# Routing attention and MLP mixer: seven block products for the second token product of two batches, the rounding's integer addition on VectorE, and the sums of the channel weights in slices

## The chip, the cores and the metric

The kernel runs on one core of one Trainium2 chip. The metric is the device time of one launch in microseconds (us), as the median of several launches. A core has a matrix engine (TensorE, "PE" in the profile; its weight loads are listed as "PEld"), a vector engine (VectorE, "DVE"), a scalar engine (ScalarE, "ACT"), GpSimd ("POOL") and a queue that issues transfers (SyncE, "SP"). Each engine works through its own list of instructions in the order of the program; semaphores hold an instruction until what it needs is done.

## The reference

Two stages, 4 batches, all in float32:

```python
# attention: 8 heads, 768 tokens, 64 per head, 16 clusters
mask   = q_assign[:, :, :, None] == k_assign[:, :, None, :]     # same cluster?
scores = np.where(mask, 0.125 * q @ k^T, -1e9)
attn   = softmax(scores) @ v                                    # (4, 8, 768, 64)
x      = attn.transpose(0, 2, 1, 3).reshape(4, 768, 512)

# mixer: w_tok1 (768, 256), w_tok2 (256, 768), w_ch1 (512, 1536), w_ch2 (1536, 512)
h  = np.maximum(x.transpose(0, 2, 1) @ w_tok1, 0.0) @ w_tok2    # over the tokens
u  = x + h.transpose(0, 2, 1)
h2 = np.maximum(u @ w_ch1, 0.0) @ w_ch2                         # over the channels
return u + h2
```

The four weights arrive as 64-bit floats and are turned into 32-bit floats on the chip ("rounding" in the kernel).

## The kernel before

The program is written in the order in which each engine executes it. Its stages: attention of 16 pairs of heads (with the rounding of `w_tok1`, `w_tok2` and `w_ch1` spread over it), the token products (with the rounding of `w_ch2`), then the channel products of the four batches.

The channel products are already done with seven block products in place of eight: both factors are cut into 2 by 2 blocks, sums and differences of blocks (`S1` to `S4` on the left, `T1` to `T4` on the right) are formed on VectorE, and seven products give the four blocks of the result. The helper that orders one chunk of it:

```python
    def chunk(n, product, done, last=False):
        def ptile(tag):                    # ps_m has 2 buffers for each tag
            return pools["ps_m"].tile([P, n], F32, tag=tag, name="p" + tag)

        X = ptile("X")
        product(X, "A11", "B11", True)
        if late:
            late.pop()()                   # the last product of the chunk before
        done("p1", X)
        Z = ptile("Z")
        product(Z, "S1", "T1", True)
        done("p5", Z)
        Y = ptile("Y")

        def product_y():
            product(Y, "A12", "B21", True)
            done("c11", Y)

        def product_z():
            product(Z, "S4", "B22", False) # on top of what stands in Z
            done("c12", Z)

        between = [product_y, product_z]
        if not last:
            between.pop(0)()
        product(X, "S2", "T2", False)      # on top of p1, once that was read
        done("u2", X)
        between.pop(0)()
        product(X, "S3", "T3", False)
        done("c22", X)
        if last:
            between.pop(0)()

        def end():
            product(X, "A22", "T4", False)
            done("c21", X)

        late.append(end)
```

A `done` reads the matmul's result out of PSUM; the next product into the same tile waits for it. The rounding of a piece of 512 columns of a weight (`raw` has the low and the high words side by side):

```python
        def scalar_part(p):                                   # ScalarE
            p["h"] = tmp("wh", U32, p["n"])
            nc.scalar.activation(out=p["h"].bitcast(F32), in_=p["hi"].bitcast(F32), func=ACT.Abs)
            p["up"] = tmp("wup", I32, p["n"])
            nc.scalar.activation(out=p["up"], in_=p["lo"], func=ACT.Copy, scale=float(2.0**-29))

        def rest(dst, p):
            h = p["h"]
            nc.vector.tensor_scalar(...)                      # L210
            nc.vector.tensor_scalar(...)                      # L215
            T = tmp("wT", U32, p["n"])                        # one buffer
            nc.vector.scalar_tensor_tensor(out=T, in0=p["hi"], ...)   # L220
            T, up = T.bitcast(I32), p["up"]
            if len(dst.shape) == 3:                           # tok2 only
                T, up = (y.rearrange("t (p j) -> t p j", j=NJ) for y in (T, up))
            nc.gpsimd.tensor_tensor(out=dst.bitcast(I32), in0=T, in1=up, op=ALU.add)   # L227
```

The token products and the sums of the left channel weights:

```python
    def tok1(b, t):
        if t == 0:
            h1s[b] = tokpool.tile([P, NT, DM], F32, name="h1", bufs=2)
        pf = mtile([P, DM], "ph1")
        for j in range(NJ):                                   # 6 matmuls, 512 wide
            nc.tensor.matmul(pf, lhsT=W["tok1"][:, j, t * P : (t + 1) * P], rhs=xs[b][:, j], ...)
        relu(h1s[b][:, t], pf)                                # VectorE and ScalarE in turn

    def tok2(b, j):
        pu = mtile([P, DM], "pu")
        for t in range(NT):                                   # 2 matmuls, 512 wide
            nc.tensor.matmul(pu, lhsT=W["tok2"][:, t, j], rhs=h1s[b][:, t], ...)
        nc.vector.tensor_tensor(out=xs[b][:, j], in0=pu, in1=xs[b][:, j], op=ALU.add)  # L539

    def left_weights():
        # A11..A22: four blocks of w_ch1, each 2 x 768 columns per partition
        yield lambda: add(A["S1"], A["A21"], A["A22"])        # 1536 elements each
        yield lambda: sub(A["S2"], A["S1"], A["A11"])
        yield lambda: sub(A["A21"], A["A11"], A["A21"])
        yield lambda: sub(A["S4"], A["A12"], A["S2"])
```

The token stage, and the first channel products:

```python
    ends = [lambda t=t: tok1(0, t) for t in range(NT)]
    for b in range(B):
        if b + 1 < B:
            ends += [lambda b=b, t=t: tok1(b + 1, t) for t in range(NT)]
        ends += [lambda b=b, j=j: tok2(b, j) for j in range(NJ)]
    # ... attention ...
    for m in range(9):
        ends.pop(0)()
        if m == 1:
            pair_put(NPAIR - 1)       # last heads' result into x, on ScalarE
            pair_out(NPAIR - 1)       # divided by the softmax sums, on VectorE
        if m % 3 == 2:
            rounding(2)
    # ...
    beside = weights + list(left_weights())
    turning = list(u_steps(0))        # u of batch 0, turned, for the channel products
    while ends:
        for _ in range(-(-len(beside) // len(ends))):
            beside.pop(0)()
        ends.pop(0)()
        if len(ends) < 18 and turning:
            turning.pop(0)()
    u_sums()                          # T1..T4 of u, on VectorE
    # ...
    beside = list(right_weights())    # four sums of w_ch2, 1536 elements each
    for b in range(B):
        for part in range(2):
            for i in range(3):
                ch1_chunk(part, i)
                # ...
                for _ in range(2):
                    if beside:
                        beside.pop(0)()
            for i in range(3):
                # ...
                ch2_chunk(b, part, i)
```

Of the kernel before, what the change touches and what calls it, by code (L numbers as in the profile page):

```python
# [48 lines left out]
def kernel(  # L49
# [131 lines left out]
    def weight_steps(pool, W, names):  # L181

        def tmp(name, dt, n):  # L190
            bufs = 1 if name == "wT" else 2
            return pool.tile([P, WMAX], dt, tag=name, name=name, bufs=bufs)[:, 0:n]

        def load_bits(src, p):
            n = p["n"] = src.shape[1]
            raw = pool.tile([P, WMAX, 2], U32, tag="raw", name="raw", bufs=3)[:, 0:n]
            nc.sync.dma_start(raw.rearrange("p n two -> p (n two)"), src.bitcast(U32))
            p["lo"], p["hi"] = raw[:, :, 0], raw[:, :, 1]

        def scalar_part(p):  # L200
# [9 lines that stand above are left out]
            nc.vector.tensor_scalar(  # L210
                out=h.bitcast(F32), in0=h.bitcast(F32), scalar1=TINY, scalar2=HUGE,
                op0=ALU.max, op1=ALU.min,
            )

            nc.vector.tensor_scalar(  # L215
                out=h, in0=h, scalar1=0x07FFFFFF, scalar2=3,
                op0=ALU.bitwise_and, op1=ALU.logical_shift_left,
            )
            T = tmp("wT", U32, p["n"])
            nc.vector.scalar_tensor_tensor(  # L220
                out=T, in0=p["hi"], scalar=0xC0000000, in1=h,
                op0=ALU.bitwise_and, op1=ALU.bitwise_or,
            )
            T, up = T.bitcast(I32), p["up"]
            if len(dst.shape) == 3:
                T, up = (y.rearrange("t (p j) -> t p j", j=NJ) for y in (T, up))
            nc.gpsimd.tensor_tensor(out=dst.bitcast(I32), in0=T, in1=up, op=ALU.add)  # L227

        pieces = list(weight_pieces(W, names))
        parts = [{} for _ in pieces]  # L230
        for i in range(len(pieces) + 2):

            def step(i=i):
                if 2 <= i:
                    rest(pieces[i - 2][0], parts[i - 2])
                if 1 <= i <= len(pieces):
                    scalar_part(parts[i - 1])
                if i < len(pieces):
                    load_bits(pieces[i][1], parts[i])

            yield step
# [262 lines left out]
        state.pop(g)  # L504


    turns = [0, 0]

    def relu(dst, src):
        turns[0] += 1  # L510
        if turns[0] % 2:
            nc.vector.tensor_scalar_max(out=dst, in0=src, scalar1=0.0)
        else:
            nc.scalar.activation(out=dst, in_=src, func=ACT.Relu)

    def mtile(shape, name):
        turns[1] += 1
        return pools["ps_m"].tile(shape, F32, tag="XZ"[turns[1] % 2], name=name)

    h1s = {}  # L520

# [4 lines that stand above are left out]
        for j in range(NJ):  # L526
            nc.tensor.matmul(  # L527
                pf, lhsT=W["tok1"][:, j, t * P : (t + 1) * P], rhs=xs[b][:, j],
                start=(j == 0), stop=(j == NJ - 1),
            )  # L530
        relu(h1s[b][:, t], pf)

    def tok2(b, j):
        pu = mtile([P, DM], "pu")
        for t in range(NT):
            nc.tensor.matmul(  # L536
                pu, lhsT=W["tok2"][:, t, j], rhs=h1s[b][:, t], start=(t == 0), stop=(t == NT - 1)
            )
        nc.vector.tensor_tensor(out=xs[b][:, j], in0=pu, in1=xs[b][:, j], op=ALU.add)  # L539

# [12 lines left out]
    def left_weights():  # L555

        w = W["ch1"]
        half = DCH // 2
        A = {
            f"A{i + 1}{j + 1}": w[:, 2 * j : 2 * j + 2, half * i : half * i + half]  # L560
            for i in range(2)
            for j in range(2)
        }
        extra = pools["wsums"].tile([P, 3, 2, half], F32, name="w1s")
        A["S1"], A["S2"], A["S4"] = (extra[:, i] for i in range(3))
        yield lambda: add(A["S1"], A["A21"], A["A22"])
        yield lambda: sub(A["S2"], A["S1"], A["A11"])
        yield lambda: sub(A["A21"], A["A11"], A["A21"])
        yield lambda: sub(A["S4"], A["A12"], A["S2"])
        A["S3"] = A["A21"]  # L570
        pools["A"] = A

    def right_weights():

        w = W["ch2"]
        B_ = {
            f"B{i + 1}{j + 1}": w[:, 6 * i : 6 * i + 6, 256 * j : 256 * j + 256]
            for i in range(2)
            for j in range(2)
        }  # L580
        extra = pools["wsums"].tile([P, 3, NCT // 2, DM // 2], F32, name="w2s")
        B_["T1"], B_["T2"], B_["T4"] = (extra[:, i] for i in range(3))
        yield lambda: sub(B_["T1"], B_["B12"], B_["B11"])
        yield lambda: sub(B_["T2"], B_["B22"], B_["T1"])
        yield lambda: sub(B_["B12"], B_["B12"], B_["B22"])
        yield lambda: sub(B_["T4"], B_["B21"], B_["T2"])
        B_["T3"] = B_["B12"]
        pools["B"] = B_
# [45 lines left out]
    def chunk(n, product, done, last=False):  # L634


        def ptile(tag):
# [5 lines that stand above are left out]
            late.pop()()  # L643
# [11 lines that stand above are left out]
            product(Z, "S4", "B22", False)  # L655
# [6 lines that stand above are left out]
        product(X, "S2", "T2", False)  # L662
# [9 lines that stand above are left out]
            done("c21", X)  # L672

        late.append(end)

    def ch1_chunk(part, i):

# [160 lines left out]

    begin()
    weights = list(weight_steps(stage, W, ("tok1", "tok2", "ch1")))  # L840
    ends = [lambda t=t: tok1(0, t) for t in range(NT)]
    for b in range(B):
        if b + 1 < B:
            ends += [lambda b=b, t=t: tok1(b + 1, t) for t in range(NT)]
        ends += [lambda b=b, j=j: tok2(b, j) for j in range(NJ)]

    def route_on(g):
        route(g)
        route_big(g)
# [46 lines left out]

    ps_sc_stack.close()
    pools["ps_m"] = pool("ps_m", 2, space=PSUM)
    for m in range(9):
        ends.pop(0)()  # L900
        if m == 1:
            pair_put(NPAIR - 1)
            pair_out(NPAIR - 1)
        if m % 3 == 2:
            rounding(2)
    assert not state
    attention.close()
    pools["wsums"] = pool("wsums", 1, side="right")
    pools["u"] = pool("upool", 1, side="right")
    beside = weights + list(left_weights())  # L910
    turning = list(u_steps(0))
    while ends:
        for _ in range(-(-len(beside) // len(ends))):
            beside.pop(0)()
        ends.pop(0)()
        if len(ends) < 18 and turning:
            turning.pop(0)()
    u_sums()
    staging.close()
    tokens.close()  # L920
    pools["mlp"] = pool("mlp", 1)
    beside = list(right_weights())
    for b in range(B):
        for part in range(2):
            for i in range(3):
                ch1_chunk(part, i)
                if part == 1 and b + 1 < B:
                    if i == 0:
                        turning = list(u_steps(b + 1))
                    if i < 2:  # L930
                        turning.pop(0)()
                for _ in range(2):
                    if beside:
                        beside.pop(0)()
            for i in range(3):
                if b == B - 1 and part == 1 and i == 2:
                    both = fits_load()
# [226 lines left out]
```

## Time and profile before

| | |
|---|---|
| time, median of 3 | 845.06 us (844.65 to 845.54) |
| profiled execution | 843.0 us |
| attention, 0 to 318 us | TensorE busy 314.87 us of it |
| token products, 318 to 401.5 us | TensorE busy 82.75 us of 83.5 |
| channel products of batch 0, 401.5 to 456 us | TensorE busy 54.14 us of 54.5, VectorE 30.10 us |
| the rest, 456 to 843 us | TensorE busy 381.25 us of 387 |
| VectorE over the whole span | busy 501.5 us (59%) |

A line of the groups reads: line of the program, engine, operation, what it writes and reads with shapes, the count; then total busy time and mean duration of one in ns; then the idle time of the engine before them, and what ended it. One float32 matmul is two records of TensorE, which overlap. A line of the timeline reads: start in us, length in us, engine, line, operation, operands, count, and in brackets how long the engine had been idle and what released it.

### The profile page before, as it was taken

The numbers are of one execution on the slowest core, as the hardware profiler recorded it, in microseconds if no ns is written. First come the engines' busy times: TensorE is split into PE (matmuls) and PEld (weight loads), VectorE is DVE, ScalarE is ACT, GpSimd is POOL, SyncE is SP. The second block draws the span as 40 slices with busy tenths as digits, with TensorE's granted clock in tenths as the row PEclk, the third lists the DMA queues.
The fourth block names the chain that finished last, engine by engine and source line by source line (L and its number), as shares of the span: only waits on it lengthen the run. The fifth ranks groups of instructions, "written<-read, shape, count | busy, mean of one in ns | idle before, by whom it ended". The sixth has DMA issues, their size and how long they took to land.

```text
span 843.0 us, 10784 instructions
## 1 busy us (share of the span) xinstructions
PE 833.0 (99%) x4102; PEld 506.3 (60%) x4102; DVE 501.5 (59%) x848; ACT 375.0 (44%) x570; POOL 45.7 (5%) x40
## 2 busy tenths in 40 slices
PE   8999999999999999999999999999999999999997
PEld 4444444444444444444577686785876867768676
DVE  6879898989898862893653434423454333443342
ACT  5678677777777762453210352103612035220210
POOL 1001010101101000330000000000000000000000
PEclk9999999999999999999999999999999999999999
DMA  9887566867775312541000050000310012200001
GB/s 152 152 149 150 114 138 136 164 129 156 149 134 122 57 44 71 170 101 28 0 1 1 19 107 26 0 1 19 87 46 0 1 19 47 85 1 0 1 17 63
DMA packets 183963, 60.19 MB, mean 71 GB/s; under 512 B 172768, under 2 KB 176864, under 8 KB 183904
## 3 DMA queue, kind: packets, MB, share of 16 engines
q1 hardware_dynamic: 182304, 59.04, 33.2%
q8 instruction: 34, 0.56, 0.3%
q10 hardware_dynamic: 1600, 0.39, 0.2%
q14 instruction: 25, 0.20, 0.1%
HBM read 34.64 MB, written 6.29 MB: 49 GB/s over the span
## 4 chain that ended last, share of the span: by engine, by line
PE 92%; DVE 6%; issue 0%; ACT 0%; DMA 0%; DVEq 0%
PE sc L422 18%; PE pX L740 15%; PE pX L689 15%; PE av L447 13%; PE pZ L689 7%; PE pZ L740 7%; PE ph L527 4%; PE pY L740 4%; PE pY L689 4%; PE pu L536 3%; PE small L483 1%; DVE wh L215 1%; PE small L302 1%; DVE wT L220 1%; DVE wh L210 1%; DVE sum L437 1%
## 5 line engine op out<-in xcount | busy, mean ns | idle before, releaser
L429 ACT ACTIVATE ex<-sc 128x768 f32<-128x768 f32 x192 | 149.2, 812 | 27.6 <-PE sc L422 16.1
L422 PE MATMUL sc<-qkT 64*128 64x384 f32 x768 | 155.1, 482 | 0.0
L437 DVE TENSOR_TENSOR sum<-sum,ex 128x768 f32<-128x768 f32 x128 | 127.7, 997 | 27.4 <-ACT ex L429 15.2
L447 PE MATMUL av<-ex,va 128*64 128x384 f32 x768 | 127.4, 488 | 0.0
L447 PEld LDWEIGHTS av<-ex,va 128*64 128x64 f32 x768 | 53.7, 137 | 71.7 <-issue 67.9
L422 PEld LDWEIGHTS sc<-qkT 64*128 64x128 f32 x768 | 68.4, 187 | 36.3 <-issue 35.5
L697 ACT COPY p<-pX 128x384 f32<-128x384 f32 x24 | 11.4, 475 | 139.5 <-PE pX L689 121.2
L689 PE MATMUL pX<-uT,wc 128*128 128x384 f32 x192 | 67.4, 487 | 0.0
L422 PE MATMUL sc<-ohT 64*128 64x384 bf16 x384 | 63.3, 324 | 0.5 <-DVE ohT L394 0.2
L689 PEld LDWEIGHTS pX<-uT,wc 128*128 128x128 f32 x192 | 36.2, 190 | 24.7 <-issue 1.0
L454 ACT COPY avrows<-av 128x768 uint16<-128x768 uint16 x32 | 25.5, 798 | 47.1 <-PE av L447 47.1
L227 POOL TENSOR_TENSOR wc<-wT,wup 128x512 int32<-128x512 int32 x24 | 33.0, 1376 | 191.3 <-DVE wT L220 191.3
L527 PE MATMUL ph<-x,wt 128*128 128x512 f32 x96 | 41.9, 594 | 0.8 <-DVE x L539 0.8
L610 ACT COPY uT<-ucols 128x768 uint16<-128x768 uint16 x32 | 33.7, 1052 | 19.7 <-DMA ucols<-urows 19.7
L536 PE MATMUL pu<-h,wt 128*128 128x512 f32 x96 | 41.7, 592 | 0.0
L422 PEld LDWEIGHTS <-ohT 64*128 64x128 bf16 x384 | 20.1, 94 | 35.9 <-issue 11.1
L553 DVE TENSOR_TENSOR c<-pZ,u 128x384 f32<-128x384 f32 x24 | 13.4, 557 | 46.9 <-PE pZ L689 46.9
L708 ACT ACTIVATE hA<-hA 128x384 f32<-128x384 f32 x24 | 12.6, 523 | 63.4 <-DVE hA L553 63.4
L553 DVE TENSOR_TENSOR x<-pX,x 128x256 f32<-128x256 f32 x24 | 10.2, 423 | 42.8 <-PE pX L740 42.8
L689 PE MATMUL pZ<-uTs,w1s 128*128 128x384 f32 x96 | 35.0, 487 | 0.4 <-DVE uTs L550 0.4
L740 PE MATMUL pX<-wc,hA 128*128 128x256 f32 x144 | 35.0, 379 | 0.0
L740 PE MATMUL pZ<-w2s,hS 128*128 128x256 f32 x144 | 35.0, 379 | 0.0
(121 smaller groups left out, 1222.3 us busy)
## 6 DMA issues: line engine op xcount, KB each, us to landing
raw<-in_moe_w_ch_dram SPq DMA_DIRECT2D x24, 512.0 KB, 4.2
va<-in_v_dram SPq DMA_DIRECT2D x16, 384.0 KB, 3.6
out_dram<-x SPq DMA_DIRECT2D x24, 256.0 KB, 2.2
qk<-in_k_dram SPq DMA_DIRECT2D x60, 96.0 KB, 3.9
qk<-in_q_dram SPq DMA_DIRECT2D x60, 96.0 KB, 3.5
raw<-in_moe_w_tok_dram SPq DMA_DIRECT2D x3, 512.0 KB, 4.3
raw<-in_moe_w_tok_dram SPq DMA_DIRECT2D x4, 384.0 KB, 3.8
ucols<-urows SPq DMA_TRANSPOSE x32, 2.8
```

Source lines behind the costliest of these rows:

```text
L227: nc.gpsimd.tensor_tensor(out=dst.bitcast(I32), in0=T, in1=up, op=ALU.add)
L422: nc.tensor.matmul(sc[:, h, 0:HS], lhsT=src[rows, 1, j], rhs=src[rows, 0, js], start=start, stop=not start,)
L429: nc.scalar.activation(out=ex, in_=sc[:, :, 0:HS], func=ACT.Exp, scale=SM_SCALE)
L437: nc.vector.tensor_tensor(out=acc, in0=acc if j > 1 else st["ex", qh, 0], in1=st["ex", qh, j], op=ALU.add)
L447: nc.tensor.matmul(av[h * D : (h + 1) * D], lhsT=st["va"][:, h, j], rhs=ex[:, h], start=(j == 0), stop=(j == NJ - 1),)
L454: nc.scalar.copy(out=st["rows"][:, qh], in_=av.bitcast(U16).rearrange("p (t w) -> p w t", w=2))
L527: nc.tensor.matmul(pf, lhsT=W["tok1"][:, j, t * P : (t + 1) * P], rhs=xs[b][:, j], start=(j == 0), stop=(j == NJ - 1),)
L536: nc.tensor.matmul(pu, lhsT=W["tok2"][:, t, j], rhs=h1s[b][:, t], start=(t == 0), stop=(t == NT - 1))
L553: nc.vector.tensor_tensor(out=dst, in0=a, in1=b, op=ALU.add)
L610: nc.scalar.copy(out=out, in_=pools.pop(("ucols", i)).rearrange("p w j t -> p w (j t)"))
L689: nc.tensor.matmul(psum, lhsT=A[a][:, k, c * P : (c + 1) * P], rhs=R[r][:, k], start=start and k == 0, stop=k == 1, skip_group_check=not s ...
L740: nc.tensor.matmul(psum, lhsT=h2[a][:, k, i * P : (i + 1) * P], rhs=Bw[w][:, 3 * part + k], start=start and k == 0, stop=k == 2, skip_grou ...
```

## The change

It does three things.

- **The second token product.** The output of two batches is cut into 2 by 2 blocks (halves of the tokens by the two batches), the inner dimension of 256 into two, and the product is done with seven block products in place of eight, through the `chunk` helper. It is meant to save matmuls. For it, sums of the blocks of `w_tok2` are formed once (`token_weights`) and sums of the two batches' hidden layers for each pair of batches (`token_sums`). Both batches' first products now stand ahead of the second, and the relu is on ScalarE alone.
- **The rounding's integer addition** is on VectorE in place of GpSimd, except for `w_tok2`. It is meant to keep the two engines out of each other's way.
- **The sums of `w_ch1`** are formed in slices of 128 columns: the first during the second token product, the other five between the chunks of batch 0's channel products. They are meant to leave VectorE free in the token stage.

```diff
             T, up = T.bitcast(I32), p["up"]
+            engine = nc.vector
             if len(dst.shape) == 3:
+                engine = nc.gpsimd
                 T, up = (y.rearrange("t (p j) -> t p j", j=NJ) for y in (T, up))
-            nc.gpsimd.tensor_tensor(out=dst.bitcast(I32), in0=T, in1=up, op=ALU.add)
+            engine.tensor_tensor(out=dst.bitcast(I32), in0=T, in1=up, op=ALU.add)
...
-        relu(h1s[b][:, t], pf)
-
-    def tok2(b, j):
-        pu = mtile([P, DM], "pu")
-        for t in range(NT):
-            nc.tensor.matmul(
-                pu, lhsT=W["tok2"][:, t, j], rhs=h1s[b][:, t], start=(t == 0), stop=(t == NT - 1)
-            )
-        nc.vector.tensor_tensor(out=xs[b][:, j], in0=pu, in1=xs[b][:, j], op=ALU.add)
+        nc.scalar.activation(out=h1s[b][:, t], in_=pf, func=ACT.Relu)
...
+    def left_sums(A, part):
+        a = {name: part(x) for name, x in A.items()}
+        yield lambda: add(a["S1"], a["A21"], a["A22"])
+        yield lambda: sub(a["S2"], a["S1"], a["A11"])
+        yield lambda: sub(a["S3"], a["A11"], a["A21"])
+        yield lambda: sub(a["S4"], a["A12"], a["S2"])
+
+    def left_chunk(c):
+        return left_sums(pools["A"], lambda x: x[:, :, c * P : (c + 1) * P])
+
+    def token_weights():
+        w = W["tok2"]
+        A = pools["AT"] = {
+            f"A{i + 1}{j + 1}": w[:, j, HJ * i : HJ * i + HJ] for i in range(2) for j in range(2)
+        }
...
+        return left_sums(A, lambda x: x)
+
+    def token_sums(b, t):
+        R = pools["RT"] = {f"B{j + 1}{k + 1}": h1s[b + k][:, j] for j in range(2) for k in range(2)}
...
+        if t == 0:
+            sub(R["T1"], R["B12"], R["B11"])
+        else:
+            sub(R["T2"], R["B22"], R["T1"])
+            sub(R["T3"], R["B22"], R["B12"])
+            sub(R["T4"], R["B21"], R["T2"])
...
+    def tok2_chunk(b, i):
+        A, R = pools["AT"], pools["RT"]
...
+        to = {"p1": "c11", "p5": "c22", "u2": "c12"}
+
+        def product(psum, a, r, start):
+            nc.tensor.matmul(psum, lhsT=A[a][:, i], rhs=R[r], start=start, stop=True, ...)
+
+        def done(name, psum):
+            x = u[to.get(name, name)]
+            add(x, psum, x)
+
+        chunk(DM, product, done, i == HJ - 1)
+        if i == HJ - 1:
+            late.pop()()
...
+    others = weights
+    for b in (0, 2):
+        for i in range(2):
+            for t in range(NT):
+                tok1(b + i, t)
+                if (b, i) == (2, 0):
+                    turning.pop(0)()
+                if (b, i, t) == (0, 0, 1):
+                    pair_put(NPAIR - 1)
+                    pair_out(NPAIR - 1)
...
+                    for sums_of in token_weights():
+                        sums_of()
+                if i == 1:
+                    if t == 0:
+                        token_sums(b, 0)
+                    beside((2, 1)[t])             # steps of the rounding
+                    if t == 1:
+                        token_sums(b, 1)
+                else:
+                    beside(1 if b == 0 else (2, 2)[t])
+                if (b, i) == (2, 1):
+                    turning.pop(0)()
+        for i in range(HJ):
+            tok2_chunk(b, i)
+            if b == 0 and i == HJ - 1:
+                turning = list(u_steps(0))
+            if b == 2:
+                for _ in range(2):
+                    turning.pop(0)()
+                if i == 1:
+                    left_weights()
+                    others = list(left_chunk(0))
+                if i >= 1:
+                    beside(2)
     u_sums()
...
+    others = list(right_weights())
...
                 ch1_chunk(part, i)
...
-                for _ in range(2):
-                    if beside:
-                        beside.pop(0)()
+                if b == 0:
+                    c = 3 * part + i + 1
+                    for sums_of in left_chunk(c) if c < NCT // 2 else ():
+                        sums_of()
+                    beside(min(len(others), 1 + (i == 1)))
```

## The prediction

> **What bounds the kernel now.** I read the page's busy times first, then the stages by windows, then the groups of the token products, and last the timeline around the hand-overs that the change touches.
>
> ```profile
> PE 833.0 (99%) x4102; PEld 506.3 (60%) x4102; DVE 501.5 (59%) x848; ACT 375.0 (44%) x570; POOL 45.7 (5%) x40
> ```
>
> The windows, with the busy time of TensorE, its weight loads, VectorE, ScalarE and GpSimd in each, then the granted clock:
>
> ```profile
> 318.00:401.50 83.50, 82.75 (x194) 36.48 (x194) 52.19 (x71) 33.02 (x47) 15.44 (x12) 1.00 0.36 93
> 401.50:456.00 54.50, 54.14 (x207) 38.85 (x206) 30.10 (x50) 8.48 (x18) 0.00 (x0) 1.00 0.00 0
> ```
>
> TensorE is busy 99% of the span, also within the token stage and batch 0's channel products, at the full granted clock (1.00). So time goes only if TensorE gets fewer matmuls, and every new wait of TensorE is paid in full.
>
> ```profile
> L527 PE MATMUL ph<-x,wt 128*128 128x512 f32 x96 | 41.9, 594 | 0.8 <-DVE x L539 0.8
> L536 PE MATMUL pu<-h,wt 128*128 128x512 f32 x96 | 41.7, 592 | 0.0
> ```
>
> 96 records of the second product are 48 matmuls. The timeline steps 1.715 us from one eviction to the next, for two matmuls: 0.858 us each. The stage needs 96 x 0.858 = 82.3 us and runs from 317.93 to 401.46: only 1.2 us of it is lost.
>
> ```profile
> 329.03 1.95 ACT L472 COPY x<-avcols 128x768 uint16<-128x768 uint16 x2
> ...
> 330.10 0.56 DVE L498 TENSOR_TENSOR x<-x,rcps 128x384 f32<-128x384 f32 x1 [6.02 <-ACT x L472]
> ...
> 361.31 0.42 DVE L210 TENSOR_SCALAR wh<-wh 128x512 f32<-128x512 f32 x1
> 361.53 1.32 POOL L227 TENSOR_TENSOR wc<-wT,wup 128x512 int32<-128x512 int32 x1 [1.67 <-DVE wT L220]
> 361.76 1.37 DVE L215 TENSOR_SCALAR wh<-wh 128x512 uint32<-128x512 uint32 x1
> ```
>
> Two things to see. The division of the last heads (L498) cannot start before 330.10, 12.2 us into the stage, as ScalarE first does the relu of the product before it. And while GpSimd adds, a VectorE instruction of 0.43 us takes 1.37 us.
>
> ```profile
> 402.26 0.95 DVE L550 TENSOR_TENSOR uTs<-uT 128x768 f32<-128x768 f32 x1
> ...
> 403.27 1.56 PE L689 MATMUL pZ<-uTs,w1s 128*128 128x384 f32 x4 [0.36 <-DVE uTs L550]
> ...
> 415.70 0.55 DVE L550 TENSOR_TENSOR hS<-hA,hS 128x384 f32<-128x384 f32 x1
> 416.17 0.55 DVE L553 TENSOR_TENSOR hA<-pY,p 128x384 f32<-128x384 f32 x1
> ...
> 417.18 0.46 ACT L697 COPY u<-pX 128x384 f32<-128x384 f32 x1
> 417.69 2.23 PEld L689 LDWEIGHTS pX<-uT,wc 128*128 128x128 f32 x8 [0.58 <-ACT u L697]
> ```
>
> These give the hand-overs. TensorE starts 0.05 us after VectorE's end (403.21 to 403.27), and the first matmul after a wait costs some 0.1 us more (its four records take 1.39 us to the next product, not 1.29). VectorE starts 0.2 us after a product's end. The last lines show that sums put among the channel chunks already cost a little: two of 1.75 us delay VectorE, ScalarE's copy behind it, and TensorE by 0.13 us.
>
> **What the Trainium skill says.** "GPSIMD Engine Reference", 4.1 Engine selection, says that GpSimd adds 32-bit integers exactly and natively. On VectorE it needs another way: "DVE: scalar operands, raw-bit mode, write accounting and state across instructions", 2. Raw-bit mode, says that uint16 streams are zero-extended and that additions below 2^24 are exact. That fits the changed program's instruction list, where the addition stands as one special instruction of 1024 elements for 512 words. No trace here has it yet. "VectorE: DVE Perf Modes", Mode 2×_1P, allows two 16-bit results per cycle to two-input instructions; if that holds, my estimate is that it costs what L220, with two inputs of 512, costs: 0.69 us. If not, 768-wide additions at 0.954 us and 384-wide at 0.557 us give 1.03 ns per element, so 1024 elements about 1.22 us. "SBUF — State Buffer", Who interferes with whom, says that GpSimd shares a port pair with VectorE and that the second to issue blocks; the trace agrees (1.37 against 0.43 us).
>
> **The change, part by part.**
>
> *Matmuls removed.* Two pairs of batches, three chunks, seven products of one matmul: 42 in place of 48. 6 x 0.858 = -5.1 us. Most of the stage's 1.2 us of losses goes too: -1.0 us. Together -6.1 us.
>
> *The integer addition.* 12 + 3 pieces in attention, 12 in the token stage. A piece is then 0.45 + 0.51 + 0.62 (start to start, timeline) + about 0.62 = 2.2 us of VectorE. Before, back to back, it blocked for 0.76 to 0.95 us at each piece, so the swap is near even. In attention the first addition of a pair of heads falls where VectorE waits for TensorE's sums anyway (idle 1.45 us at 298.15). I count 0 there.
>
> *Entry to the first pair's second product.* The fourth product goes on top of the first (`S2 x T2` into X), so it needs X's eviction by VectorE, and the program puts that behind all of this: division 1.4 (ends 13.6, counted from 317.93), sums of `w_tok2` 4 x 0.56 (15.9), piece 1 (18.1), T1 0.65 (18.7), pieces 2, 3, 4 (25.3), T2 to T4 (27.2), eviction 0.69 (27.9). VectorE cannot begin earlier, since the division waits until 12.2. TensorE has done 24 matmuls at 20.6 and three products at 23.15. It waits +4.8 us.
>
> *Entry for the second pair*, counted from the end of the first pair's products. ScalarE, in order, does part of each piece between its relus, so pieces 6 to 8 end at 15.5; T1 waits for the third relu and ends at 16.95; pieces 9, 10, 11 end at 23.55, T2 to T4 at 25.45, the eviction at 26.1. TensorE is ready at 23.15: +3.0 us.
>
> *Within the chunks.* A product is one matmul of 0.858 us. `S3 x T3` waits for the eviction of u2 with one product between: 0.2 + 0.69 + 0.05 + 0.1 = 1.04 us, so 0.18 lost; the last product of a chunk, behind c22, likewise. Six such waits per pair are 1.1 us. In the last chunk, `S2 x T2` comes without Y ahead of it, and X's eviction stands behind c21's: another 0.8. Two pairs: +3.8 us.
>
> *Sums of u.* Two slice sums of 128x256 (0.43 each, from slope and 0.16 fixed) stand between the last eviction and T1 of u: TensorE waits 1.4 us in place of 0.4, +1.0 us.
>
> *Channel chunks of batch 0.* From the timeline, S2 of the hidden layer ends 2.5 us after a chunk's `S3 x T3`. Then four slice sums (1.75) and the sums of `w_ch2` (1.75 each) follow. The next chunk's third product needs slice sum S1: ready at 2.98 against 2.58, so 0.5 with the restart, after chunks 0, 1, 3, 4. After chunk 1 two sums of `w_ch2` follow: VectorE is free at 7.8, c11 at 8.9, ScalarE's relu 9.4 and copy 9.86, where TensorE would be at 8.2: another 1.75. After chunk 2 the first ch2 chunk needs its p1 at 5.2 and gets it at 6.95: 1.9. Sum 4 x 0.5 + 1.75 + 1.9 = 5.65, less 0.7 that the same stage loses before: +4.9 us.
>
> *Sum:* -6.1 + 4.8 + 3.0 + 3.8 + 1.0 + 4.9 = +11.4 us, 856.4 us. The serial count takes every wait at its full length, and later waits may absorb earlier ones. I take 855.
>
> **The rivals.** (1) VectorE keeps up and the saved matmuls show: 839 to 841 us. For it: VectorE is busy only 52 of 83.5 us in this stage, and six evictions of 0.69 us fit into a chunk of six us. Against it: its work stands in bursts just ahead of what TensorE needs, and the start at 12.2 is fixed. (2) The addition takes 1.22 us: pieces 1 to 4 add 2.1 us to the first entry and 9 to 11 1.6 us to the second, and attention, where VectorE is busy 129.5 of 153 us, may begin to wait: 860 to 866. For it: 1024 elements in the list. (3) The end of the port conflict speeds up attention. Against it: TensorE is busy 152.71 of 153 us from 165 to 318, so there is nothing to gain; 845 at most less a few tenths.
>
> **Range and chances.** 855, with 846 to 861 to hold it 8 times in 10: the low end is two thirds of my waits, roughly, going away; the high end is rival 2. 2% is 17 us, which only rival 2 passes. Faster by over 2% would need more than the 6 matmuls can give. Chances: 0.01 faster, 0.94 within, 0.05 slower.
>
> **What would show it.** In the changed kernel, second-product matmuls with 84 records; TensorE idle before pX in the token stage, released by VectorE, in one gap near 341 us and one some 40 to 45 us later; the new addition's mean duration (0.69 or 1.22); TensorE waits on slice sums in batch 0's channel chunks; attention ending near 318. If the token stage is shorter than 80 us, or VectorE has no backlog at its first eviction, the prediction is wrong at the entries. If batch 0's channel stage stays at 54.5 us, it is wrong there.

## The result and the profile after

The changed kernel takes 868.52 us (median of 6 runs, 866.71 to 869.02) against 845.05 us before: a ratio of 1.0274, 95% interval 1.026 to 1.0287. The profiled executions span 866.8 and 843.0 us, 23.8 us apart. The prediction was 855 us with 846 to 861: the direction held, and more than half of the size was missing.

The busy times of the changed kernel's page:

```profile
PE 838.2 (97%) x4090; PEld 502.8 (58%) x4090; DVE 525.0 (61%) x921; ACT 378.5 (44%) x574; POOL 8.3 (1%) x13
```

TensorE has 12 records fewer (six matmuls), and yet is busy 5 us longer. So some of its matmuls have become slower, besides the time in which it stands still. The windows of the token stage show where (busy time of TensorE, its weight loads, VectorE, ScalarE, GpSimd, then TensorE's granted clock):

```profile
318.00:340.00 22.00, 22.00 (x71) 9.48 (x68) 9.36 (x19) 8.87 (x14) 0.00 (x0) 1.00 0.32 92
340.00:402.00 62.00, 48.94 (x103) 19.74 (x103) 41.49 (x72) 19.77 (x31) 0.00 (x0) 0.92 0.27 80
402.00:424.00 22.00, 20.45 (x42) 7.88 (x41) 15.21 (x25) 7.08 (x9) 0.00 (x0) 0.91 0.19 37
```

The clock, 1.00 in both windows of the kernel before, is 0.92 and 0.91 on average here. What TensorE waited for, over the whole execution (total, times, longest):

```profile
PE pX L703 <- DVE x L541: 12.9, 4, 7.4
PE sc L425 <- DVE sim L321: 3.3, 5, 0.8
...
PE pX L780 <- DVE p L541: 1.2, 1, 1.2
PE pZ L729 <- DVE uTs L538: 1.0, 1, 1.0
PE pX L729 <- ACT u L737: 0.9, 1, 0.9
PE pZ L703 <- DVE h1s L538: 0.7, 1, 0.7
```

L703 is the token product, L541 its eviction, L425 the attention scores, L780 and L729 the channel products. The groups by form, of the first product, the new addition and the product that waits:

```profile
L523 PE MATMUL ph<-x,wt 128*128 128x512 f32 x96 | 41.6, 593 | 0.0
...
L230 DVE CUSTOM_DVE_ANT_0 wc<-wT,wup 128x1024 uint16<-128x1024 uint16 x24 | 16.6, 692 | 2.1
...
L703 PE MATMUL pX<-h1s,wt2s 128*128 128x512 f32 x12 | 8.4, 793 | 12.9 <-DVE x L541 12.9
```

The addition takes 0.69 us, as estimated. The first product's matmuls are unchanged (593 ns), while the product behind the wait has a mean of 793 ns.

By the first matmul of each stage, the 23.8 us divide like this, up to rounding. (In the front of this document, the stretch of 401.5 to 456 us is called batch 0's channel products. It is the first half of them, one of two parts; the second half runs to 510 us.)

| stage, by TensorE's first matmul in it | before | after | difference |
|---|---|---|---|
| start to first token product | 317.93 | 321.70 | +3.8 |
| token products | 83.53 | 99.08 | +15.6 |
| batch 0, first half | 54.02 | 57.71 | +3.7 |
| batch 0, second half | 54.50 | 55.39 | +0.9 |
| the rest | 333.0 | 332.9 | -0.1 |

The first entry in the timeline of the changed kernel:

```profile
333.87 0.56 DVE L501 TENSOR_TENSOR x<-x,rcps 128x384 f32<-128x384 f32 x1 [8.90 <-ACT x L475]
...
344.12 1.02 PE L703 MATMUL pY<-h,wt 128*128 128x512 f32 x2
...
346.46 0.69 DVE L230 CUSTOM_DVE_ANT_0 wc<-wT,wup 128x1024 uint16<-128x1024 uint16 x1
...
348.87 0.69 DVE L541 TENSOR_TENSOR x<-pX,x 128x512 f32<-128x512 f32 x1
...
349.61 2.08 PE L703 MATMUL pX<-h1s,wt2s 128*128 128x512 f32 x2 [4.47 <-DVE x L541]
351.48 1.91 PE L703 MATMUL pZ<-h,wt2s 128*128 128x512 f32 x2
353.19 2.64 PE L703 MATMUL pX<-h,wt 128*128 128x512 f32 x4
```

The division at 333.87 is 12.2 us into the stage; the eviction ends at 349.56, 27.9 us into it: both as worked out. TensorE's third product is over at 344.97 (0.858 us after its start), and the fourth starts at 349.61. But then each product takes 1.7 us, not 0.86, until about 355.

### The profile page after: what moved, and what is told of

It reads as the page before. It is cut to its first block, busy times and chain, and to the rows that moved or that the text cites. A ratio compares the mean times of both kernels' runs of the same rounds, so it can differ in the third digit from the quotient of the medians.

```text
span 866.8 us, 10800 instructions
## 1 busy us (share of the span) xinstructions
PE 838.2 (97%) x4090; PEld 502.8 (58%) x4090; DVE 525.0 (61%) x921; ACT 378.5 (44%) x574; POOL 8.3 (1%) x13
## 4 chain that ended last, share of the span: by engine, by line
PE 70%; DVE 19%; ACT 3%; DMA 3%; issue 2%; SPq 2%; DVEq 0%; POOL 0%; ACTq 0%; POOLq 0%
PE pX L780 14%; PE pX L729 13%; PE sc L425 9%; PE pZ L780 7%; PE pZ L729 7%; PE av L450 5%; DVE sum L440 5%; PE pY L780 3%; PE pY L729 3%; PE pX L703 3%; DVE qkT L295 2%; ACT ex L432 2%; PE ph L523 2%; DVE wT L220 2%; DMA raw<-in_moe_w_ch_dram 1%
## 5 line engine op out<-in xcount | busy, mean ns | idle before, releaser
L432 ACT ACTIVATE ex<-sc 128x768 f32<-128x768 f32 x192 | 151.1, 811 | 31.4 <-PE sc L425 19.9
L425 PE MATMUL sc<-qkT 64*128 64x384 f32 x768 | 155.1, 482 | 0.0
L440 DVE TENSOR_TENSOR sum<-sum,ex 128x768 f32<-128x768 f32 x128 | 123.3, 963 | 26.8 <-ACT ex L432 14.6
L425 PEld LDWEIGHTS sc<-qkT 64*128 64x128 f32 x768 | 68.0, 187 | 37.6 <-issue 37.3
L737 ACT COPY p<-pX 128x384 f32<-128x384 f32 x24 | 11.4, 475 | 140.1 <-PE pX L729 121.8
L729 PE MATMUL pX<-uT,wc 128*128 128x384 f32 x192 | 67.4, 487 | 0.9 <-ACT u L737 0.9
L425 PE MATMUL sc<-ohT 64*128 64x384 bf16 x384 | 62.8, 324 | 3.5 <-DVE sim L321 3.3
L541 DVE TENSOR_TENSOR x<-pX,x 128x512 f32<-128x512 f32 (+1 forms) x48 | 26.4, 556 | 54.0 <-PE pX L780 42.8
L729 PEld LDWEIGHTS pX<-uT,wc 128*128 128x128 f32 x192 | 36.3, 190 | 25.4 <-ACT u L737 1.5
L541 DVE TENSOR_TENSOR c<-pZ,u 128x384 f32<-128x384 f32 x24 | 13.4, 558 | 47.3 <-PE pZ L729 46.3
L425 PEld LDWEIGHTS <-ohT 64*128 64x128 bf16 x384 | 18.7, 94 | 39.7 <-issue 9.4
L729 PE MATMUL pZ<-uTs,w1s 128*128 128x384 f32 x96 | 35.4, 491 | 1.7 <-DVE uTs L538 1.0
L780 PE MATMUL pX<-w2s,hS 128*128 128x256 f32 x144 | 35.1, 380 | 1.2 <-DVE p L541 1.2
L780 PE MATMUL pX<-wc,hA 128*128 128x256 f32 x144 | 35.0, 379 | 0.0
L780 PE MATMUL pZ<-w2s,hS 128*128 128x256 f32 x144 | 35.0, 379 | 0.0
L780 PE MATMUL pY<-wc,hA 128*128 128x256 f32 x144 | 35.0, 379 | 0.0
```

Of the source, the lines that this page charges most:

```text
L425: nc.tensor.matmul(sc[:, h, 0:HS], lhsT=src[rows, 1, j], rhs=src[rows, 0, js], start=start, stop=not start,)
L432: nc.scalar.activation(out=ex, in_=sc[:, :, 0:HS], func=ACT.Exp, scale=SM_SCALE)
L440: nc.vector.tensor_tensor(out=acc, in0=acc if j > 1 else st["ex", qh, 0], in1=st["ex", qh, j], op=ALU.add)
L541: nc.vector.tensor_tensor(out=dst, in0=a, in1=b, op=ALU.add)
L729: nc.tensor.matmul(psum, lhsT=A[a][:, k, c * P : (c + 1) * P], rhs=R[r][:, k], start=start and k == 0, stop=k == 1, skip_group_check=not s ...
L780: nc.tensor.matmul(psum, lhsT=h2[a][:, k, i * P : (i + 1) * P], rhs=Bw[w][:, 3 * part + k], start=start and k == 0, stop=k == 2, skip_grou ...
```

## The experiments

In these groups of runs the kernel before had medians of 845.2 to 845.5 us. What an experiment saves is counted from the changed kernel's 868.52.

### 1 and 2: the integer addition in attention

The first puts the addition back on GpSimd for the weights that are rounded during attention:

```diff
             engine = nc.vector
+            if p.get("pool"):
+                engine = nc.gpsimd
...
-        parts = [{} for _ in pieces]
+        parts = [{"pool": names[0] == "tok1" and len(names) == 3} for _ in pieces]
```

> The changed kernel, with the rounding's integer addition back on GpSimd for the weights rounded during attention (w_tok1, w_ch1); w_ch2's additions stay on VectorE. Theory A: in attention the addition on VectorE stands between the rounding and the transposition that frees the PSUM tile of the sums, so TensorE's third score product waits 0.6 to 0.8 us per pair of heads (3.3 us in the trace). Then attention ends near 318 us again and the time falls by 3.5 to 4 us, to about 865. Rival: the 3.8 us come from elsewhere (a different layout of tiles, later loads): then the time stays within 0.5 us of 868.5.

Measured: 865.24 us (864.03 to 865.76), 3.3 us less, a little under the 3.5 to 4 expected. The first token product starts at 318.10, not 321.70. The five waits of the scores are down to one of 0.2 us:

```profile
PE sc L427 <- DVE sim L323: 0.2, 1, 0.2
```

The second is the kernel before with this part alone:

```diff
-            nc.gpsimd.tensor_tensor(out=dst.bitcast(I32), in0=T, in1=up, op=ALU.add)
+            engine = nc.gpsimd if len(dst.shape) == 3 else nc.vector
+            engine.tensor_tensor(out=dst.bitcast(I32), in0=T, in1=up, op=ALU.add)
```

> The kernel before, with only the integer addition moved to VectorE (w_tok2 stays on GpSimd). Theory A: attention loses the same 3.8 us, and the token stage, where VectorE no longer blocks behind GpSimd, gains at most 1 us: 848 to 849. Rival: freeing VectorE of the port conflict pays: 844 to 845.

Measured: 848.99 us (848.89 to 849.05), ratio 1.0043 (1.0029 to 1.0057): 3.6 us more than the kernel before. In its profile the token stage starts 3.3 us later than there (321.23 against 317.93) and is 0.9 us longer (84.41 against 83.53), so the end of the conflict with GpSimd brought no gain there. What TensorE waited for in attention:

```profile
PE sc L423 <- DVE sim L319: 3.3, 5, 0.8
```

The same 3.3 us in five waits appear with the addition on VectorE and go with it. The mechanism can be read off one pair of heads. In the kernel before:

```profile
203.77 0.69 DVE L220 SCALAR_TENSOR_TENSOR wT<-raw,wh 128x512 uint32<-128x512 uint32 x1
...
204.38 0.58 DVE L487 STREAM_TRANSPOSE dent<-small 128x384 f32<-128x384 f32 x1
204.60 1.27 POOL L227 TENSOR_TENSOR wc<-wT,wup 128x512 int32<-128x512 int32 x1 [13.51 <-DVE wT L220]
204.88 0.54 DVE L318 STREAM_TRANSPOSE sim<-small 128x384 f32<-128x384 f32 x1
```

And in the changed kernel, for the same pair:

```profile
206.36 0.69 DVE L230 CUSTOM_DVE_ANT_0 wc<-wT,wup 128x1024 uint16<-128x1024 uint16 x1
206.97 0.57 DVE L490 STREAM_TRANSPOSE dent<-small 128x384 f32<-128x384 f32 x1
207.47 0.54 DVE L321 STREAM_TRANSPOSE sim<-small 128x384 f32<-128x384 f32 x1
...
208.07 0.34 PE L425 MATMUL sc<-ohT 64*128 64x384 bf16 x2 [0.58 <-DVE sim L321]
```

The transposition `sim` frees one of three PSUM tiles for the next scores. GpSimd's addition ran beside it; on VectorE it stands ahead of it, and TensorE's third score product waits. The changed kernel has this order in nine pairs of heads; in five of them TensorE waits, 0.58 to 0.78 us each.

### 3: matmuls in the waits

```diff
         def product(psum, a, r, start):
+            if i == 0 and a == "S2":
+                pw = ps_av.tile([P, P], F32, tag="av", name="pw")
+                for _ in range(70 if b == 0 else 125):
+                    nc.tensor.matmul(pw, lhsT=identb, rhs=identb, start=True, stop=True)
             nc.tensor.matmul(...)
```

> The changed kernel, with 70 and 125 bf16 matmuls of 128x128 that nothing reads, placed just ahead of the first S2 x T2 of the two pairs, where TensorE stands still for 4.6 and 7.5 us. They add work but should end before the wait does. Theory B: the two waits also cost because the granted clock falls to a half for the next 4 to 5 us (0.50 in the windows after them); with TensorE kept at work the clock stays at 1.00 and 2.5 us come back at each: 863 to 864. Rival: the low clock has another cause (the matmuls' own pattern), or the products after the wait are slow because of their evictions: 868 to 869.

Measured: 863.49 us (863.27 to 864.02), 5.0 us less with more work. The windows of this kernel after the first wait, and of the changed kernel there:

```profile
346.00:350.00 4.00, 3.43 (x49) 2.89 (x47) 3.98 (x7) 0.25 (x1) 0.00 (x0) 1.00 0.13 52
350.00:354.00 4.00, 4.00 (x10) 1.42 (x10) 2.39 (x4) 0.00 (x0) 0.00 (x0) 1.00 0.00 0
```

```profile
349.60:354.80 5.20, 5.19 (x6) 2.14 (x7) 2.54 (x4) 0.00 (x0) 0.00 (x0) 0.51 0.00 0
401.10:405.70 4.60, 4.59 (x6) 1.96 (x7) 2.53 (x4) 3.49 (x4) 0.00 (x0) 0.50 0.47 89
```

With TensorE kept at work the clock stays at 1.00. From the start of `S2 x T2` to the next chunk's second product the changed kernel takes 7.10 and 6.95 us (first and second pair), this one 4.78 and 4.79: 2.3 and 2.2 us are the price of the low clock.

### 4: pieces of rounding ahead of the division

```diff
                 tok1(b + i, t)
+                if (b, i, t) == (0, 0, 0):
+                    beside(3)
...
                     if t == 0:
                         token_sums(b, 0)
-                    beside((2, 1)[t])
+                    if b == 2:
+                        beside((2, 1)[t])
```

> The changed kernel, with three of the four pieces of rounding that stand between the division of the last heads and the first pair's second product moved ahead of the division, where VectorE is idle for 8.9 us. Theory C: TensorE's first wait is VectorE's backlog behind the division; it shrinks from 4.6 us to under 1 us, and with it goes the half clock: 868.5 - 4 - 2.5 = 861.5 to 862.5. Rival: the wait is for something else (the relus on ScalarE, the loads), or the moved pieces are late too as their loads and ScalarE parts are not there: 866 to 868.5.

Measured: 861.90 us (861.71 to 862.44), 6.6 us less. Its timeline:

```profile
335.07 0.69 DVE L230 CUSTOM_DVE_ANT_0 wc<-wT,wup 128x1024 uint16<-128x1024 uint16 x1
336.61 0.56 DVE L501 TENSOR_TENSOR x<-x,rcps 128x384 f32<-128x384 f32 x1 [0.85 <-ACT x L475]
...
345.32 0.68 DVE L541 TENSOR_TENSOR x<-pX,x 128x512 f32<-128x512 f32 x1
...
346.06 1.12 PE L703 MATMUL pX<-h1s,wt2s 128*128 128x512 f32 x2 [0.65 <-DVE x L541]
```

Three of the four pieces now fill the time in which VectorE was idle, and idle time ahead of the division falls from 8.90 to 0.85 us. TensorE's wait falls from 4.47 to 0.65 us, and the products after it run at full clock.

### 5: loads ahead of the turning

The second wait was 7.4 us, where I had counted 3.0. Its timeline in the changed kernel:

```profile
384.01 1.21 SPq L617 DMA_TRANSPOSE ucols<-urows  x1
385.31 1.48 SPq L197 DMA_DIRECT2D raw<-in_moe_w_ch_dram  x3
...
389.26 0.67 ACT L203 ACTIVATE wh<-raw 128x512 f32<-128x512 f32 x1 [4.11 <-DMA raw<-in_moe_w_ch_dram]
...
390.38 0.59 ACT L527 ACTIVATE h<-ph 128x512 f32<-128x512 f32 x1
...
391.00 0.69 DVE L538 TENSOR_TENSOR h1s<-h,h 128x512 f32<-128x512 f32 x1 [3.95 <-ACT h L527]
...
401.11 2.07 PE L703 MATMUL pX<-h1s,wt2s 128*128 128x512 f32 x2 [7.38 <-DVE x L541]
```

A load of raw weights (L197) stands behind a turning of `u` (L617), which itself waits for a copy on ScalarE. ScalarE then waits 4.11 us for the load, and the relu (L527) stands behind it, although its product was over some 5 us before. VectorE stands idle for 3.95 us until that relu. The experiment moves the steps of the rounding ahead of the turning:

```diff
                 tok1(b + i, t)
-                if (b, i) == (2, 0):
-                    turning.pop(0)()
...
                     beside(1 if b == 0 else (2, 2)[t])
-                if (b, i) == (2, 1):
+                if b == 2:
                     turning.pop(0)()
```

> The changed kernel, with one swap in the program: between the second pair's first two first products, the steps of the rounding (load, ScalarE part) now stand ahead of the turning of batch 0's u, whose DMA waits for ScalarE and holds up the loads behind it in SyncE's queue. Theory D: the second wait is longer than the 3.0 us I counted because the pieces come late: the load of a piece waits in SyncE's queue behind a DMA transposition, ScalarE waits for the load, and the relu behind it. With the loads ahead the wait of 7.4 us falls to 3 to 3.5 us: 868.5 - 4.3 = about 864, and 861.5 if the clock stays up as well. Rival: the loads are late for lack of buffers or of bandwidth: 867.5 to 868.5.

Measured: 863.30 us (863.02 to 864.27), 5.2 us less. The second wait:

```profile
395.18 2.08 PE L703 MATMUL pX<-h1s,wt2s 128*128 128x512 f32 x2 [3.71 <-DVE x L541]
```

It is 3.7 us, a little over the 3 to 3.5 expected, and the wait for T1 has gone; the clock still falls to 0.50 after it. One load still issues behind a turning here (at 385.44), and ScalarE waits 3.47 us for it, so a part of the lateness is left. Some 0.8 us of what its profile gains came by luck, at the first wait (experiment 10).

### 6: the slice sums in idle time

```diff
-    def ch1_chunk(part, i):
+    def ch1_chunk(part, i, slices=False):
...
                 add(a, psum, kept["p1"])
                 nc.scalar.activation(out=a, in_=a, func=ACT.Relu)
+                for sums_of in left_chunk(c + 1) if slices and c + 1 < NCT // 2 else ():
+                    sums_of()
...
-                ch1_chunk(part, i)
+                ch1_chunk(part, i, b == 0)
...
-                    c = 3 * part + i + 1
-                    for sums_of in left_chunk(c) if c < NCT // 2 else ():
-                        sums_of()
-                    beside(min(len(others), 1 + (i == 1)))
+                    beside(min(len(others), 2))
```

> The changed kernel, with the slice sums of w_ch1 for the next chunk placed behind the eviction c11, where VectorE waits some 2 us for the next product, in place of behind the hidden layer's sums; the sums of w_ch2 two behind chunk 0 and two behind chunk 1, as in the kernel before. Theory E: in batch 0 the sums cost 4.6 us over the kernel before (3.7 in the first half with the 0.7 of u's sums, 0.9 in the second) by their place, not by their amount: 3 to 3.8 us come back, 864.8 to 865.5. Rival: VectorE is short of time there whatever the order: 867.5 or more.

Measured: 863.68 us (862.64 to 864.84), 4.8 us less; 3 to 3.8 were expected. In its profile batch 0's halves take 54.64 and 54.50 us, where the changed kernel takes 57.71 and 55.39 and the kernel before 54.02 and 54.50: 4.0 us. The difference to 4.8 lies within the spread of these runs. The same sums cost TensorE 0.6 us where VectorE would wait for the next product anyway, and 4.6 us in the place that the change gave them. The 0.6 us are those of u's first sum, behind two of the first chunk's slice sums, which stay where they were.

### 7: two products between

The token product gets its own copy of `chunk`, called `token_chunk`. Shown against `chunk`, with the rest cut:

```diff
         X = ptile("X")
         product(X, "A11", "B11", True)
-        if late:
-            late.pop()()
         done("p1", X)
         Z = ptile("Z")
         product(Z, "S1", "T1", True)
         done("p5", Z)
+        if late:
+            late.pop()()
         Y = ptile("Y")
+        product(X, "S2", "T2", False)
+        done("u2", X)
+        product(Y, "A12", "B21", True)
+        done("c11", Y)
...
```

> The changed kernel, with another order of the products within a chunk of the token product: X1, Z1, X4 of the chunk before, X2, Y, Z2, X3, and p1's eviction queued at once. Two products (1.7 us) then lie between any product and the one that must wait for its eviction (1.04 us), but for the last chunk. Theory F: six waits of 0.18 us and one of 0.8 us per pair are for want of a second product between; 1.3 to 1.6 us per pair come back: 865.5 to 866. In the two entries the first wait may start one product earlier and swallow up to 0.9 us each of it, without need of more. Rival: the evictions themselves are too slow for seven in six us: 868 or more.

Measured: 866.80 us (866.14 to 868.28), 1.7 us less; expected were 2.5 to 3. Its two waits at the entries:

```profile
349.11 2.08 PE L703 MATMUL pX<-h1s,wt2s 128*128 128x512 f32 x2 [5.32 <-DVE x L541]
...
400.19 2.07 PE L703 MATMUL pX<-h1s,wt2s 128*128 128x512 f32 x2 [8.24 <-DVE x L541]
```

Within the chunks the waits have gone but for those of each pair's last chunk. The entries took part of it back: Y no longer stands ahead of `S2 x T2`, so the two waits grew from 4.47 and 7.38 to 5.32 and 8.24 us, one product each, as VectorE's backlog ends when it did.

### 8 and 9: all of it mended

The eighth combines experiments 1, 4, 5, 6 and 7, with the second pair's pieces ahead of its T1 as well. It forms the first slice of `w_ch1` one chunk earlier. Its edits beyond those five:

```diff
+                if (b, i, t) == (2, 0, 0):
+                    beside(3)
                 tok1(b + i, t)
...
-                    beside((2, 1)[t])
...
-                if i == 1:
+                if i == 0:
                     left_weights()
                     others = list(left_chunk(0))
-                if i >= 1:
+                if i <= 1:
                     beside(2)
```

> All of it together: integer additions on GpSimd in attention and on VectorE in the token stage, pieces ahead of the division and, for the second pair, ahead of T1, loads ahead of the turning, the new order within token chunks, slice sums in idle slots (the first chunk's one token chunk earlier). If the four causes are the whole difference, what is left is the saving of six products and of the old stage's 1.2 us, less 1 to 2.5 us of rest in the two entries: 840.5 to 843.5, below the kernel before (845.35). Rival: a further wait appears that the others hid (ScalarE, whose pieces now come in bursts between the relus): 845 to 850.

Measured: 843.22 us (842.85 to 845.16), ratio 0.9978 (0.997 to 0.9985), as expected. What was left in the token stage were the two entries:

```profile
PE pX L705 <- DVE x L543: 3.0, 2, 1.5
```

The ninth frees them. T3 and T4 of the hidden layer move behind the first evictions, and the first chunk has Y ahead of `S2 x T2` again:

```diff
             sub(R["T2"], R["B22"], R["T1"])
-            sub(R["T3"], R["B22"], R["B12"])
-            sub(R["T4"], R["B21"], R["T2"])
...
             add(x, psum, x)
+            if i == 0 and name == "p5":
+                sub(R["T3"], R["B22"], R["B12"])
+            if i == 0 and name == "u2":
+                sub(R["T4"], R["B21"], R["T2"])
...
+        if first:                          # the first chunk of a pair
+            product_y()
         product(X, "S2", "T2", False)
         done("u2", X)
-        product(Y, "A12", "B21", True)
-        done("c11", Y)
+        if not first:
+            product_y()                    # product_y as in chunk
```

> The mended kernel of the run before (843.2), with the two entries freed as well: T3 and T4 of the hidden layer are formed only after the first chunk's p1 and u2 evictions, and in the first chunk Y stands ahead of S2 x T2 again. The two waits of 1.5 us that are left there should end: T2 and the eviction then end 2.2 us after the last first product, and TensorE needs them at 2.57. Expected 840 to 841, that is the kernel before less the six products (5.15) and little else. Rival: ScalarE's relu or T3 is late in its new place: 842 to 843.

Measured: 840.36 us (840.29 to 840.67), as expected, against 845.16: ratio 0.9944 (0.993 to 0.9957), 4.8 us less than the kernel before. The windows of its token stage and of batch 0's first half:

```profile
318.50:397.40 78.90, 78.66 (x185) 33.79 (x182) 63.11 (x109) 34.42 (x51) 0.00 (x0) 1.00 0.37 99
397.40:451.40 54.00, 53.64 (x205) 38.51 (x204) 33.91 (x61) 8.49 (x18) 0.00 (x0) 1.00 0.00 0
```

TensorE is busy 78.66 of 78.9 us, at the full clock. VectorE does as much here as in the changed kernel, 63.1 us against 62.3, in a token stage of 78.9 us against 99.1. 90 matmuls of 0.858 us are 77.2 us, so 1.7 us are still lost in the stage; of the 5.1 us that six products are worth, the kernel gains 4.8.

### 10: how long a wait the clock bears

```diff
-                for _ in range(70 if b == 0 else 125):
+                for _ in range(35 if b == 0 else 75):
```

> The changed kernel with 35 and 75 of the dummy matmuls, so that of the two waits of 4.6 and 7.5 us some 2.6 and 3.1 us are left idle. Theory B says that the clock falls with the length of the idle time: waits of 0.65 and 1.5 us left it at 1.00, waits of 3.7 us and more took it to 0.50. What happens in between is open; if both waits keep the clock the time is 863 to 864, if both lose it 868.

Measured: 867.39 us, one run. The timeline and the windows after the waits:

```profile
349.13 1.92 PE L707 MATMUL pX<-h1s,wt2s 128*128 128x512 f32 x2 [2.53 <-DVE x L541]
...
400.55 2.08 PE L707 MATMUL pX<-h1s,wt2s 128*128 128x512 f32 x2 [3.20 <-DVE x L541]
```

```profile
350.00:352.00 2.00, 2.00 (x4) 0.83 (x3) 0.96 (x2) 0.00 (x0) 0.00 (x0) 0.50 0.00 0
```

Waits of 2.53 and 3.20 us were already enough for the half clock. With 0.65 (experiment 4) and 1.50 us (experiment 8) it stayed. From the start of `S2 x T2` to the next chunk's second product this kernel takes 6.28 and 6.25 us, so the half clock costs it 1.5 us at each wait, not 2.2 or 2.3.

The length of a wait does not settle this price. Wherever the clock stands at 0.50 in the twelve profiles, from 10 us on to the last product, it does so for 3.41, 6.83 or 10.24 us: one, two or three steps of 3.41 us. In each profile all changes of the clock lie on one grid of that step. I laid this grid over TensorE's matmuls. Each stretch of 3.41 us at full clock in which TensorE was idle for 59% or more (2.0 us) was followed by one at 0.50; with up to 57% (1.9 us) the clock stayed. The wait of 2.53 us filled 74% of one stretch. The grid does not stand still against the program: the first wait is 4.47 us in the changed kernel and in experiment 5, but 6.83 us at 0.50 follow in the one profile and 3.41 us in the other, and the price is 2.3 us in the one and 1.5 us in the other. That is luck, and it is a part of the spread of the changed kernel's runs: the run of 866.71 us has a mean clock of 0.994, that of 869.02 us one of 0.988.

## Why the prediction was right or wrong

| step | predicted, us | measured, us |
|---|---|---|
| six matmuls and the old stage's losses | -6.1 | -6.3 |
| integer addition, attention | 0 | +3.8 |
| first entry | +4.8 | +4.6 |
| second entry | +3.0 | +8.4 |
| half clock after the entries | not counted | +4.5 |
| within the chunks | +3.8 | +4.4 |
| u's sums and channel chunks of batch 0 | +5.9 | +4.6 |
| sum | +11.4 | +23.8 |

The measured column is read from the two timelines: a wait is the start of a product less the end of the one before it; the second entry has the wait for T1 in it; the clock's part is from experiment 3; "within the chunks" is what then remains of 21.9 us lost in the token stage (99.08 less 90 x 0.858). The first row is 77.2 less 83.53 and so holds by count. The rows add up to 24.0; the rest of the kernel has -0.1, and the remainder is rounding.

The mechanism, TensorE waiting for VectorE's backlog, was right. Three terms failed: the attention counted as 0, the second entry, and the half clock that was not in the sum. They are 3.8, 5.4 and 4.5 us too low, together 13.7; the other terms were 1.1 us too high.

*Matmuls removed* and *Entry to the first pair* held, the latter to 0.2 us, and experiments 9 and 4 confirm them. As an exchange within the token stage the addition was near even, as told: experiment 2 has it at +0.9 us.

*The integer addition* failed in "I count 0 there". I had read one idle gap, at 298.15, before the sums of the last pair of heads but one. That pair routes no later pair, and so has no transposition `sim` behind the addition. In nine earlier pairs the addition stands ahead of the transposition that frees a PSUM tile, and in five of them TensorE waits. Experiments 1 and 2 show it: attention is 3.6 us shorter without the addition on VectorE and 3.3 us longer with it. "Attention ending near 318" failed with it: it ends at 321.7.

*Entry for the second pair* failed in "pieces 6 to 8 end at 15.5; T1 waits for the third relu and ends at 16.95". I followed VectorE's and ScalarE's lists, but not SyncE's. There the loads stand behind the turning of `u`, so T1 ended at 391.7, which is 22.3 us into the stage, and TensorE waited 8.4 us in all. Experiment 5 shows it: with the loads ahead, 3.7 us are left.

*The half clock* was missing altogether. "TensorE: Matmul & The Clock Gate", What's actually happening, in the Trainium skill says that the clock falls to a half after an idle window of about 3.4 us and comes back after a busy one, and that these windows run on by themselves and do not start with the kernel. My own sum had a wait of 4.8 us in it, and I took it at its length alone. The traces agree on the half clock and on windows of 3.41 us that the program does not set. They differ on the idle window: 2.0 us of idle time within one were enough here, so a wait of 2.53 us was; the measurement decides. Experiment 3 shows the cost, 4.5 us for both waits. The closing guess, that "later waits may absorb earlier ones", had the sign wrong here: after both long waits the products took twice as long.

*Within the chunks* was right in kind and 0.6 us short. *Sums of u* was right in kind: 1.03 us of waiting in place of 0.36, so +0.7 and not +1.0. *Channel chunks of batch 0* was right in kind and too dear: four slice sums take 1.47 us of VectorE from start to start, not 1.75 (they overlap), and the waits after chunks 1 and 2 were 0.9 and 1.16 us where I had 1.75 and 1.9. In the timeline of the changed kernel:

```profile
447.96 0.46 ACT L737 COPY u<-pX 128x384 f32<-128x384 f32 x1
...
448.48 1.56 PE L729 MATMUL pX<-uT,wc 128*128 128x384 f32 x4 [0.90 <-ACT u L737]
...
456.37 1.56 PE L780 MATMUL pX<-w2s,hS 128*128 128x256 f32 x6 [1.16 <-DVE p L541]
```

Of the rivals, the first (VectorE keeps up) was false for this kernel; the ninth experiment reaches its 839 to 841 us with the same products, another order of VectorE's work, and the additions of attention back on GpSimd. Its count of six evictions in a chunk is one too low: each of the seven products has one, 4.8 us of VectorE in 6.0. The second was false: the addition takes 0.69 us. So it was wrong, too, that "only rival 2 passes" 2%: three missed costs passed it without. The third was false: attention became 3.8 us longer.

## What to carry to other kernels

When an engine bound at 99% gets work whose release depends on a helper engine, count what stands ahead of the releasing instruction in every queue on its way, the DMA queue included, and in the tightest repetition, not in the one that the timeline happens to show. In these runs every wait of TensorE of 2.53 us or more was followed by a low clock, which cost 1.5 to 2.3 us where it was worked out; a sum of waits needs a term for it, and in a kernel with such waits a difference of a microsecond or two may be the luck of the grid. An integer addition, or a sum, costs by its place: in the token stage VectorE works 63.1 us in the ninth experiment and 62.3 us in the changed kernel, and the stage is 20 us shorter.

## What the runs showed of the hardware

- After waits of 2.53, 3.20, 3.71, 4.47 and 7.38 us TensorE's granted clock was 0.50 for 3.41 or 6.83 us; after 0.65 and 1.50 us it stayed at 1.00. It changed on a grid of 3.41 us: a stretch with 2.0 us or more of idle time was followed by one at 0.50, with 1.9 us or less it stayed. Small bf16 matmuls of 128x128 in waits of 4.6 and 7.5 us held it at 1.00 (experiment 3).
- A 32-bit integer addition of 512 words per partition takes 0.69 us on VectorE, as long as a two-input instruction of 512 float32 elements, and 1.26 to 1.86 us on GpSimd in the kernel before (mean 1.38). One of 1.32 us on GpSimd held a VectorE instruction of 0.43 us up to 1.37 us.
